# A fused transform and SwiGLU kernel: split value units from tile 3 on, the earlier order of a unit, and a broadcast row by TensorE

## The chip, the cores and the metric

The kernel runs on one core of one Trainium2 chip. The metric is the device time of one execution in microseconds (us). Five engines work side by side: TensorE (matmuls; PE in the profile, with its weight loads as PEld), VectorE (DVE), ScalarE (ACT), GpSimd (POOL) and SyncE (SP), which issues most of the transfers. [...]

## The reference

Eight batches of 3008 rows of 256 numbers go through a two-dimensional Fourier transform, of which the real part is kept. Each of the 24064 resulting rows then goes through a SwiGLU block with 1536 hidden columns:

```python
X = np.fft.fft(np.fft.fft(x, axis=1), axis=2).real      # x: (8, 3008, 256)
t = X.reshape(24064, 256)
g = t @ w_gate                                          # (256, 1536)
silu = g * (1.0 / (1.0 + np.exp(-g)))
out = (silu * (t @ w_val)) @ w_out                      # (1536, 256)
```

## The kernel before

**Mirror pairs.** The real part of the transform of row k and of row M - k consist of the same two parts, P and Q, once added and once subtracted. The kernel keeps P and Q (128 numbers each per token, since the weights take in the transform along the columns) and computes two output rows from each column of them, a plus row and a mirrored row. It folds the weights into Wp (for P), Wq (for Q) and Wm, which is -2 times Wq except in row 0. For the plus row it adds Wp.P and Wq.Q in one PSUM bank; adding Wm.Q on top gives the mirrored row in the same bank.

**Tiles and units.** The 12032 columns are cut into 24 tiles of mostly 512 columns (`wide`; tiles 0 and 3 have 480, the last one 320). A tile has 12 units, one for each 128 hidden columns (`f`). So there are 288 units, which the main loop (L874) runs over. A unit makes the gate `g` and the value `v` for the plus rows, multiplies silu(g) with v into `hp`, adds the mirror to both, and multiplies again into `hm` (with the columns reversed).

**Plain and split units.** In a plain unit the gate and the value have one bank each, TensorE runs six matmuls of 512 columns, and DVE makes both products (L755, L785). In a split unit the value is left in two parts, e (Wp.P) and o (Wm.Q), in two banks. DVE makes the values of both rows from them in three steps (L744, L746, L748); the first adds row 0 of Q, broadcast over the partitions (`bc`) and weighted by `w0`. GpSimd makes the products (L749, L773). A split unit has five matmuls of 512 columns. `split(u)` (L703) picks the units: from tile 2 to the last tile but one, f in (0, 2, 3, 5, 7, 9), and nine of twelve in tiles 21 and 22.

**Output.** The rows of a finished tile are multiplied with `w_out` while the next tile is computed: 96 matmuls of 256 columns (L675, `OWork`), eight for each unit, in two groups of four. ScalarE copies each finished pair of blocks (L681), SP stores it.

**Order of a unit, from tile 1 on** (L896 to L904): `gate_b` of the unit ahead (mirror of the gate, its silu; GpSimd's product, if split), four output matmuls, `gate_a` of this unit, `value_b` of the unit ahead (mirror of the value and product, if plain), `value_a` of this unit, four output matmuls. Tile 0 has the order of the changed kernel.

**Buffers.** [...]three for gates (`psG`), three for values (`psV`), two for outputs (`psO`). GpSimd's products have four buffers for silu results (`sgv`) and four for values (`vv`).

**Folding and transforms beside it.** GpSimd folds the rows of the next batches (L147 to L174; SDf, EOf, Af, CE, BB), in steps laid out by unit number in `seq` (L796 to L805): batch 1 in units 6 to 24, batches 2 and on from unit 25, three folds in about 62 units at first. Their loads (L128 to L141) go out three to a unit on SP. A step follows, in GpSimd's order, the products of its unit. The transforms (`transform`, L545) of a half batch run at the end of a unit named in `slot` (L788): unit 33, which is (tile 2, f = 9), then (3, 4), (5, 4), (6, 4) and so on. Each has 16 or more matmuls, two ScalarE copies into `od` and the sums into the P and Q tiles on DVE (L579).

**Row 0 of Q.** In unit 7 (10 in tile 2) of the tile ahead, two transfers on SP write row 0 of Qt to DRAM and read it back into all partitions (L881, L882).

Of the kernel before, what the change touches and what calls it, by code (L numbers as in the profile page):

```python
# [12 lines left out]
F32 = mybir.dt.float32  # L13
I32 = mybir.dt.int32
BF16 = mybir.dt.bfloat16
AF = mybir.ActivationFunctionType
Alu = mybir.AluOpType
# [14 lines left out]
def kernel(  # L32
# [8 lines left out]
    nc = tc.nc  # L41
    B, M, D = x.shape
    Dff = moe_w_gate.shape[1]
    P = 128
# [4 lines left out]
    nF = Dff // P  # L49
    T = 512  # L50
# [6 lines left out]
    nT = len(wide)  # L57
# [9 lines left out]
    def width(t):  # L67
        return wide[t]

    def tile_of(c):  # L70
        return max(t for t in range(nT) if t0[t] <= c)
# [6 lines left out]
    psG = ctx.enter_context(tc.tile_pool(name="psG", bufs=3, space=bass.MemoryType.PSUM))  # L78
# [6 lines left out]
    Wm = const.tile([P, 2, Dff], BF16, name="Wm")  # L85
# [5 lines left out]
    sel = const.tile([P, P], BF16, name="sel")  # L91
# [22 lines left out]
    def rows_at(b, row, ap):  # L114
        return bass.AP(tensor=x.tensor, offset=(b * M + row) * D, ap=ap)
# [4 lines left out]
    def down_set(b, a, j, L, n):  # L120

        return rows_at(b, R * (a + 1) - 2 * j, [[2 * L * D, n], [-2 * D, L], [1, 2 * D]])
# [107 lines left out]
    for hi in range(2):  # L230
        q.dma_start(out=XC3[64 * hi:64 * hi + NCR, 0:2, :],
                    in_=rows_at(0, 2 * (P + 1) - 1 + 2 * hi * R, [[2 * D, NCR], [R * D, 2], [1, 2 * D]]))
    for hi in range(2):
        for a in range(2):
            q.dma_start(out=XC3[64 * hi:64 * hi + NCR, 2 + a, :],
                        in_=down_set(0, 3 - 2 * hi - a, JC, LC, NC_))
    q.dma_start(out=XC0[NCR:64 + NCR + 1:64, 0:2, 1],
                in_=rows_at(0, 0, [[2 * R * D, 2], [R * D, 2], [1, D]]))
# [21 lines left out]
    for i in range(6):  # L260
        ps = psO.tile([P, T], F32, name="o")
# [99 lines left out]
    opposite(0)  # L361
    nc.vector.memset(EOf[:, 1, :, P:P + 1], 0.0)
    nc.vector.memset(Tab[:, :, :, :, NOO - 1:NOO], 0.0)
    vts(m2, pcol, scalar1=0.0, scalar2=-2.0, op0=Alu.not_equal, op1=Alu.mult)
    vts(sgn, half, scalar1=1.0 / 32, scalar2=1.0, op0=Alu.mult, op1=Alu.add)
    vts(wC, pc, scalar1=float(LC - 1), scalar2=-0.5, op0=Alu.is_equal, op1=Alu.mult)
# [146 lines left out]
    def pq_tiles(t):  # L513
        if t not in ptile:
            w = width(t) + B if t == nT - 1 else T
            ptile[t] = (pqp if t < nT - 1 else const).tile([P, w], BF16, name="Pt")
            qtile[t] = (pqp if t < nT - 1 else const).tile([P, w], BF16, name="Qt")
        return ptile[t], qtile[t]
# [78 lines left out]
    def whole_part(b, part):  # L597
        transform(b, part, (0,))
        transform(b, part, (1,))
# [15 lines left out]
    sgp = ctx.enter_context(tc.tile_pool(name="sg", bufs=3))  # L615
    sgv = ctx.enter_context(tc.tile_pool(name="sgv", bufs=4))
    esp = ctx.enter_context(tc.tile_pool(name="es", bufs=2))
    bcp = ctx.enter_context(tc.tile_pool(name="bc", bufs=2))
# [73 lines left out]
    hts = {}  # L692
    state = {}
    owork = None

    SPLIT = (0, 2, 3, 5, 7, 9)
    SPLIT_END = (0, 1, 2, 4, 5, 7, 8, 10, 11)
    t_end = tile_of((B - 1) * H) + 1

    rowd = tc.dram_tile([nT, T], BF16, name="rowd")  # L700
    bc = {}

    def split(u):  # L703

        return 2 <= u[0] < nT - 1 and u[1] in (SPLIT if u[0] < t_end else SPLIT_END)

    def gate_a(u):
        t, f = u
        w = width(t) + (B if t == nT - 1 else 0)
        fs = slice(f * P, (f + 1) * P)  # L710
        if f == 0:
            hts[t] = (hp.tile([P, nF, T + B], BF16, name="hp"), hp.tile([P, nF, T], BF16, name="hm"))
        Pt, Qt = pq_tiles(t)

        def mm(ps, Wt, gv, src, start, stop):
            nc.tensor.matmul(ps[:, :w], Wt[:, gv, fs], src[:, :w], start=start, stop=stop,  # L716
                             skip_group_check=True)

        g = psG.tile([P, T], F32, name="g")
        mm(g, Wp, 0, Pt, True, False)  # L720
        mm(g, Wq, 0, Qt, False, True)
        sg = (sgv if split(u) else sgp).tile([P, T], F32, name="sgv" if split(u) else "sg")
        nc.scalar.activation(sg[:, :w], g[:, :w], AF.Silu)  # L723
        state[u] = (g, sg)

    def value_a(u):
        t, f = u
        w = width(t) + (B if t == nT - 1 else 0)
        fs = slice(f * P, (f + 1) * P)
        Pt, Qt = pq_tiles(t)  # L730
        g, sg = state[u]

        def mm(ps, Wt, gv, src, start, stop):
            nc.tensor.matmul(ps[:, :w], Wt[:, gv, fs], src[:, :w], start=start, stop=stop,  # L734
                             skip_group_check=True)

        if split(u):
            e = psV.tile([P, T], F32, name="v")
            mm(e, Wp, 1, Pt, True, True)
            o = psV.tile([P, T], F32, name="v")  # L740
            mm(o, Wm, 1, Qt, True, True)
            stt = nc.vector.scalar_tensor_tensor
            es = esp.tile([P, T], F32, name="es")
            stt(es[:, :w], bc[t][:, :w], w0[:, f:f + 1], e[:, :w], op0=Alu.mult, op1=Alu.add)  # L744
            vp = vvp.tile([P, T], F32, name="vv")
            stt(vp[:, :w], o[:, :w], -0.5, es[:, :w], op0=Alu.mult, op1=Alu.add)  # L746
            vm = vvp.tile([P, T], F32, name="vv")
            stt(vm[:, w - 1::-1], o[:, :w], 0.5, es[:, :w], op0=Alu.mult, op1=Alu.add)  # L748
            nc.gpsimd.tensor_tensor(hts[t][0][:, f, :w], sg[:, :w], vp[:, :w], op=Alu.mult)  # L749
            state[u] = (g, vm)  # L750
            return
        v = psV.tile([P, T], F32, name="v")
        mm(v, Wp, 1, Pt, True, False)
        mm(v, Wq, 1, Qt, False, True)
        nc.vector.tensor_tensor(hts[t][0][:, f, :w], sg[:, :w], v[:, :w], op=Alu.mult)  # L755
        state[u] = (g, v)

    def mirror(u, gv, ps):
        t, f = u
        w = width(t)  # L760
        nc.tensor.matmul(ps[:, :w], Wm[:, gv, f * P:(f + 1) * P], pq_tiles(t)[1][:, :w], start=False, stop=True,  # L761
                         skip_group_check=True)

    def gate_b(u):

        t, f = u
        w = width(t)
        g, v = state[u]
        mirror(u, 0, g)
        if split(u):  # L770
            sg = sgv.tile([P, T], F32, name="sgv")
            nc.scalar.activation(sg[:, w - 1::-1], g[:, :w], AF.Silu)  # L772
            nc.gpsimd.tensor_tensor(hts[t][1][:, f, :w], sg[:, :w], v[:, :w], op=Alu.mult)  # L773
        else:
            sg = sgp.tile([P, T], F32, name="sg")
            nc.scalar.activation(sg[:, :w], g[:, :w], AF.Silu)  # L776
            state[u] = (sg, v)

    def value_b(u):
        t, f = u  # L780
        w = width(t)
        sg, v = state.pop(u)
        if not split(u):
            mirror(u, 1, v)
            nc.vector.tensor_tensor(hts[t][1][:, f, w - 1::-1], sg[:, :w], v[:, :w], op=Alu.mult)  # L785


    slot = {(b, part): max(first_tile[(b, part)] - 1, 0) * nF + 4 for b, part in jobs}  # L788
# [10 lines left out]
    for b in range(2, B, 2):  # L799
        u = slot[(b, 0)] - 1  # L800
# [8 lines left out]
    def run_loads(n):  # L809
        for _, fn in loads[:n]:  # L810
            fn()
        del loads[:n]
# [29 lines left out]
    for jb in jobs[1:]:  # L842
        u = slot[jb]
# [28 lines left out]
    prev = None  # L872
    owork = None
    for i, u in enumerate(units):  # L874
        t, f = u
        if f == (10 if t == 2 else 7) and t + 1 < nT and split((t + 1, SPLIT[0])):

            bc.pop(t - 1, None)
            bc[t + 1] = bcp.tile([P, T], BF16, name="bc")
            w = width(t + 1)  # L880
            nc.sync.dma_start(out=rowd[t + 1:t + 2, :w], in_=pq_tiles(t + 1)[1][0:1, :w])  # L881
            nc.sync.dma_start(out=bc[t + 1][:, :w], in_=rowd[t + 1:t + 2, :w].to_broadcast([P, w]))  # L882
        for fn in before.pop(i, ()):
            fn()
        if i == 10:
            loads[0:0] = ((("A", 1), fn) for fn in load_a(1, nc.sync))
        run_loads(3)

        if i < nF:
            gate_a(u)  # L890
            value_a(u)
            if prev is not None:
                gate_b(prev)
                value_b(prev)
        else:
            gate_b(prev)  # L896
            if owork:
                owork.run(4)
            gate_a(u)
            value_b(prev)  # L900
            if prev[1] == nF - 1:
                owork = OWork(prev[0], hts[prev[0]])
            value_a(u)
            owork.run(4)  # L904
        for what, j in fold_at.get(i, ()):
            fold_step(what, j, i)
        for what in act_at.pop(i, ()):
            load_next(what)
        if i in job_at:
            whole_part(*job_at[i])  # L910
        prev = u
    while owork.steps:
        owork.run(8)
    gate_b(prev)
    value_b(prev)
    owork = OWork(prev[0], hts[prev[0]])
    owork.run(len(owork.steps))

# [29 lines left out]
```

## Time and profile before

| | us |
|---|---|
| three runs | 699.02, 697.26, 696.71 |
| median | 697.26 |
| profiled execution | 699.02 |
| its span, first to last instruction | 697.2 |

| engine | busy us | share of the span |
|---|---|---|
| TensorE | 674.9 | 97% |
| TensorE weight loads | 412.4 | 59% |
| VectorE | 515.8 | 74% |
| ScalarE | 413.7 | 59% |
| GpSimd | 592.9 | 85% |

Groups (line, engine, what, form, count | busy us, mean ns of one | idle us of the engine ahead of them, and what ended it):

```profile
L749 POOL TENSOR_TENSOR hp<-sgv,vv 128x512 bf16<-128x512 f32 (+1 forms) x132 | 167.6, 1270 | 60.9 <-DVE vv L746 58.4
L785 DVE TENSOR_TENSOR hm<-sg,v 128x512 bf16<-128x512 f32 (+2 forms) x156 | 104.1, 668 | 111.9 <-PE v L761 75.8
L716 PE MATMUL g<-Pt,Wp 128*128 128x512 bf16 (+2 forms) x288 | 108.5, 377 | 0.3 <-ACT sgv L772 0.3
L153 POOL TENSOR_TENSOR SDf<-XA 128x1024 f32<-128x1024 f32 x28 | 65.9, 2360 | 2.9 <-DMA XA<-in_x_dram 2.8
```

The mean of a matmul, 377 ns, is not the time that it costs: matmuls overlap, and what counts is the distance from one start to the next. The busy share of an engine is a mean over stretches of different kind, so the tiles have to be looked at one by one.

### The profile page before, as it was taken

To read this page: it belongs to the slowest core of one execution; us is meant where nothing else is said; L and a number is where in the kernel's file an instruction comes from. 1 tells how busy PE (TensorE), PEld (TensorE's weight loads), DVE (VectorE), ACT (ScalarE), POOL (GpSimd) and SP (SyncE) were. 2 spreads that over 40 slices of the span, in tenths; PEclk is the share of its full clock that TensorE was granted. 3 is DMA by queue.
4 is the path that set the end of the run, shared out by engine and by line. 5 is a ranking of instruction groups with operands and counts; after the bars stand their busy time and mean duration, and the time that the engine had idled before them with its cause. 6 is when DMAs were issued, how large, how long until landed. Compare 5 with 4: busy or idle time off the path is not lost.

```text
span 697.2 us, 13316 instructions
## 1 busy us (share of the span) xinstructions
PE 674.9 (97%) x4348; PEld 412.4 (59%) x4348; DVE 515.8 (74%) x924; ACT 413.7 (59%) x744; POOL 592.9 (85%) x577
## 2 busy tenths in 40 slices
PE   8999879999999999999999999999999999999997
PEld 5446535566565565565665656656665556656676
DVE  8895637777777777678777787778787787788762
ACT  7675535566565566565665656655666556656663
POOL 7998988899999899999998999999899645758820
PEclk9999979999999999999999999999999999999999
DMA  9646353241512412415126111116111111101112
GB/s 223 111 72 133 99 132 91 66 129 49 157 54 71 121 54 73 118 47 166 40 62 144 54 42 44 53 40 167 39 55 46 39 36 49 54 31 55 47 46 70
DMA packets 48634, 55.33 MB, mean 79 GB/s; under 512 B 6647, under 2 KB 36532, under 8 KB 48564
## 3 DMA queue, kind: packets, MB, share of 16 engines
q1 hardware_dynamic: 45380, 52.12, 27.4%
q0 software_dynamic: 3184, 2.36, 2.5%
q8 instruction: 34, 0.56, 0.3%
q14 instruction: 36, 0.29, 0.2%
HBM read 32.14 MB, written 24.67 MB: 81 GB/s over the span
## 4 chain that ended last, share of the span: by engine, by line
PE 80%; POOL 6%; DMA 4%; issue 3%; DVE 3%; SPq 2%; ACT 1%; DVEq 0%; POOLq 0%; ACTq 0%
PE o L675 30%; PE g L716 14%; PE v L734 14%; PE g L761 8%; PE v L761 4%; DMA XA<-in_x_dram 4%; PE g L566 3%; PE v L566 3%; POOL SDf L153 2%; POOL hm L773 1%; POOL hp L749 1%; DVE vv L746 1%; DMA out_dram<-ev 1%; PE v L542 1%; PE g L542 1%
## 5 line engine op out<-in xcount | busy, mean ns | idle before, releaser
L749 POOL TENSOR_TENSOR hp<-sgv,vv 128x512 bf16<-128x512 f32 (+1 forms) x132 | 167.6, 1270 | 60.9 <-DVE vv L746 58.4
L785 DVE TENSOR_TENSOR hm<-sg,v 128x512 bf16<-128x512 f32 (+2 forms) x156 | 104.1, 668 | 111.9 <-PE v L761 75.8
L675 PE MATMUL o<-Wo,hm 128*128 128x256 bf16 (+2 forms) x1140 | 170.5, 274 | 0.0
L675 PE MATMUL o<-Wo,hp 128*128 128x256 bf16 (+2 forms) x1140 | 170.1, 273 | 0.0
L773 POOL TENSOR_TENSOR hm<-sgv,vv 128x512 bf16<-128x512 f32 (+1 forms) x132 | 167.7, 1270 | 1.7 <-ACT sgv L772 1.7
L675 PEld LDWEIGHTS <-hp 128*128 128x128 bf16 (+2 forms) x1140 | 112.0, 99 | 69.9 <-issue 14.6
L675 PEld LDWEIGHTS <-hm 128*128 128x128 bf16 (+2 forms) x1140 | 112.2, 99 | 62.5 <-issue 7.8
L776 ACT ACTIVATE sg<-g 128x512 f32<-128x512 f32 (+2 forms) x156 | 90.7, 582 | 79.7 <-PE g L761 77.8
L772 ACT ACTIVATE sgv<-g 128x512 f32<-128x512 f32 (+1 forms) x132 | 78.7, 596 | 94.2 <-PE g L761 72.5
L761 PE MATMUL g<-Qt,Wm 128*128 128x512 bf16 (+2 forms) x288 | 108.4, 376 | 12.0 <-ACT sgv L723 9.4
L716 PE MATMUL g<-Qt,Wq 128*128 128x512 bf16 (+2 forms) x288 | 108.7, 378 | 0.5 <-DVE Qt L579 0.5
L716 PE MATMUL g<-Pt,Wp 128*128 128x512 bf16 (+2 forms) x288 | 108.5, 377 | 0.3 <-ACT sgv L772 0.3
L734 PE MATMUL v<-Pt,Wp 128*128 128x512 bf16 (+2 forms) x288 | 108.8, 378 | 0.0
L755 DVE TENSOR_TENSOR hp<-sg,v 128x512 bf16<-128x512 f32 (+2 forms) x156 | 103.2, 662 | 6.8 <-ACT sg L723 5.7
L723 ACT ACTIVATE sg<-g 128x512 f32<-128x512 f32 (+2 forms) x156 | 91.5, 586 | 26.9 <-PE g L716 25.4
L746 DVE SCALAR_TENSOR_TENSOR vv<-v,es 128x512 f32<-128x512 f32 (+1 forms) x132 | 91.2, 691 | 21.9 <-POOL hp L749 4.5
L723 ACT ACTIVATE sgv<-g 128x512 f32<-128x512 f32 (+1 forms) x132 | 79.8, 604 | 34.3 <-PE g L716 22.2
L744 DVE SCALAR_TENSOR_TENSOR es<-bc,w,v 128x512 f32<-128x512 bf16 (+1 forms) x132 | 97.6, 740 | 0.3 <-PE v L734 0.3
L748 DVE SCALAR_TENSOR_TENSOR vv<-v,es 128x512 f32<-128x512 f32 (+1 forms) x132 | 89.8, 680 | 7.3 <-POOL hm L773 7.3
L153 POOL TENSOR_TENSOR SDf<-XA 128x1024 f32<-128x1024 f32 x28 | 65.9, 2360 | 2.9 <-DMA XA<-in_x_dram 2.8
L761 PE MATMUL v<-Qt,Wm 128*128 128x512 bf16 (+2 forms) x156 | 58.2, 373 | 2.0 <-DVE hp L755 2.0
L734 PE MATMUL v<-Qt,Wq 128*128 128x512 bf16 (+2 forms) x156 | 58.5, 375 | 0.0
(163 smaller groups left out, 706.8 us busy)
## 6 DMA issues: line engine op xcount, KB each, us to landing
out_dram<-ev SPq DMA_DIRECT2D x96, 128.0 KB
XA<-in_x_dram SPq DMA_DIRECT2D x32, 256.0 KB
XA<-in_x_dram SPq DMA_DIRECT2D x112, 64.0 KB
XC<-in_x_dram SPq DMA_DIRECT2D x32, 120.0 KB
XC<-in_x_dram SPq DMA_DIRECT2D x105, 32.0 KB
bc<-rowd SPq DMA_DIRECT2D x20, 128.0 KB
out_dram<-ev SPq DMA_DIRECT2D x12, 120.0 KB
out_dram<-ev SPq DMA_DIRECT2D x10, 112.0 KB
```

Of the source, the lines that this page charges most:

```text
L675: nc.tensor.matmul(ps[:n, j, :], hts[minus][:, f, c:c + n], Wo[:, f, :], start=(f == 0), stop=(f == nF - 1))
L716: nc.tensor.matmul(ps[:, :w], Wt[:, gv, fs], src[:, :w], start=start, stop=stop, skip_group_check=True)
L723: nc.scalar.activation(sg[:, :w], g[:, :w], AF.Silu)
L734: nc.tensor.matmul(ps[:, :w], Wt[:, gv, fs], src[:, :w], start=start, stop=stop, skip_group_check=True)
L744: stt(es[:, :w], bc[t][:, :w], w0[:, f:f + 1], e[:, :w], op0=Alu.mult, op1=Alu.add)
L746: stt(vp[:, :w], o[:, :w], -0.5, es[:, :w], op0=Alu.mult, op1=Alu.add)
L749: nc.gpsimd.tensor_tensor(hts[t][0][:, f, :w], sg[:, :w], vp[:, :w], op=Alu.mult)
L755: nc.vector.tensor_tensor(hts[t][0][:, f, :w], sg[:, :w], v[:, :w], op=Alu.mult)
L761: nc.tensor.matmul(ps[:, :w], Wm[:, gv, f * P:(f + 1) * P], pq_tiles(t)[1][:, :w], start=False, stop=True, skip_group_check=True)
L773: nc.gpsimd.tensor_tensor(hts[t][1][:, f, :w], sg[:, :w], v[:, :w], op=Alu.mult)
L776: nc.scalar.activation(sg[:, :w], g[:, :w], AF.Silu)
L785: nc.vector.tensor_tensor(hts[t][1][:, f, w - 1::-1], sg[:, :w], v[:, :w], op=Alu.mult)
```

## The change

The diff does four things.

1. Split units begin at tile 3 (`3 <= u[0]`). The six split units of tile 2 become plain.
2. Row 0 of Q is broadcast by a matmul: `sel`, a 128 x 128 matrix, gets ones in row 0 and zeros below; at f = 0 of each tile with split units, `sel` times the Q tile goes into a gate bank, and ScalarE copies it into `bc`, now in float32. The two transfers and the DRAM tile go.
3. The order of a unit is: gate and value of this unit (`part_a`), four output matmuls, mirrors of gate and value of the unit ahead with their silu and products (`part_b`), four output matmuls. The engines' own orders follow: on DVE the steps of this unit stand ahead of the mirrored product of the unit ahead, on GpSimd the product of this unit ahead of the mirrored one of the unit ahead, on ScalarE the silu of this unit ahead of the mirrored one of the unit ahead.
4. The pieces `gate_a`, `value_a`, `mirror`, `gate_b` and `value_b` become `part_a` and `part_b`, with the same operations in them.

```diff
+    nc.vector.memset(sel[0:1, :], 1.0)
...
-    rowd = tc.dram_tile([nT, T], BF16, name="rowd")
...
-        return 2 <= u[0] < nT - 1 and u[1] in (SPLIT if u[0] < t_end else SPLIT_END)
+        return 3 <= u[0] < nT - 1 and u[1] in (SPLIT if u[0] < t_end else SPLIT_END)
...
+    def part_a(u):
...
         g = psG.tile([P, T], F32, name="g")
         mm(g, Wp, 0, Pt, True, False)
         mm(g, Wq, 0, Qt, False, True)
...
         if split(u):
             e = psV.tile([P, T], F32, name="v")
             mm(e, Wp, 1, Pt, True, True)
             o = psV.tile([P, T], F32, name="v")
             mm(o, Wm, 1, Qt, True, True)
+            sg = sgv.tile([P, T], F32, name="sgv")
+            nc.scalar.activation(sg[:, :w], g[:, :w], AF.Silu)
...
+    def part_b(u):
...
+        for gv, ps in ((0, g), (1, v))[:1 if split(u) else 2]:
+            nc.tensor.matmul(ps[:, :w], Wm[:, gv, f * P:(f + 1) * P], Qt[:, :w], start=False, stop=True,
+                             skip_group_check=True)
         if split(u):
             sg = sgv.tile([P, T], F32, name="sgv")
             nc.scalar.activation(sg[:, w - 1::-1], g[:, :w], AF.Silu)
             nc.gpsimd.tensor_tensor(hts[t][1][:, f, :w], sg[:, :w], v[:, :w], op=Alu.mult)
+            return
+        sg = sgp.tile([P, T], F32, name="sg")
+        nc.scalar.activation(sg[:, :w], g[:, :w], AF.Silu)
+        nc.vector.tensor_tensor(hts[t][1][:, f, w - 1::-1], sg[:, :w], v[:, :w], op=Alu.mult)
...
-        if f == (10 if t == 2 else 7) and t + 1 < nT and split((t + 1, SPLIT[0])):
-
-            bc.pop(t - 1, None)
-            bc[t + 1] = bcp.tile([P, T], BF16, name="bc")
-            w = width(t + 1)
-            nc.sync.dma_start(out=rowd[t + 1:t + 2, :w], in_=pq_tiles(t + 1)[1][0:1, :w])
-            nc.sync.dma_start(out=bc[t + 1][:, :w], in_=rowd[t + 1:t + 2, :w].to_broadcast([P, w]))
+        if f == 0 and split((t, SPLIT[0])):
+            ps = psG.tile([P, T], F32, name="g")
+            w = width(t)
+            nc.tensor.matmul(ps[:, :w], sel, pq_tiles(t)[1][:, :w], start=True, stop=True)
+            bc.pop(t - 2, None)
+            bc[t] = bcp.tile([P, T], F32, name="bc")
+            nc.scalar.copy(bc[t][:, :w], ps[:, :w])
...
-        if i < nF:
-            gate_a(u)
-            value_a(u)
-            if prev is not None:
-                gate_b(prev)
-                value_b(prev)
-        else:
-            gate_b(prev)
-            if owork:
-                owork.run(4)
-            gate_a(u)
-            value_b(prev)
+        part_a(u)
+        if owork:
+            owork.run(4)
+        if prev is not None:
+            part_b(prev)
             if prev[1] == nF - 1:
                 owork = OWork(prev[0], hts[prev[0]])
-            value_a(u)
+                owork.run(4)
+        if owork and not (prev is not None and prev[1] == nF - 1):
             owork.run(4)
```

More of the change, by code (lines that the diff above doesn't have):

```diff
@@ L698 @@
     t_end = tile_of((B - 1) * H) + 1
-    rowd = tc.dram_tile([nT, T], BF16, name="rowd")
     bc = {}
     def split(u):
-        return 2 <= u[0] < nT - 1 and u[1] in (SPLIT if u[0] < t_end else SPLIT_END)
-    def gate_a(u):
+        return 3 <= u[0] < nT - 1 and u[1] in (SPLIT if u[0] < t_end else SPLIT_END)
+    def part_a(u):
         t, f = u
@@ L721, in gate_a @@
         mm(g, Wq, 0, Qt, False, True)
[L722 to L735, printed above, removed]
         if split(u):
@@ L754, in value_a @@
         mm(v, Wq, 1, Qt, False, True)
+        sg = sgp.tile([P, T], F32, name="sg")
+        nc.scalar.activation(sg[:, :w], g[:, :w], AF.Silu)
         nc.vector.tensor_tensor(hts[t][0][:, f, :w], sg[:, :w], v[:, :w], op=Alu.mult)
         state[u] = (g, v)
-    def mirror(u, gv, ps):
+    def part_b(u):
         t, f = u
         w = width(t)
[L761 to L769, printed above, removed]
+        Pt, Qt = pq_tiles(t)
+        g, v = state.pop(u)
+        for gv, ps in ((0, g), (1, v))[:1 if split(u) else 2]:
+            nc.tensor.matmul(ps[:, :w], Wm[:, gv, f * P:(f + 1) * P], Qt[:, :w], start=False, stop=True,
+                             skip_group_check=True)
         if split(u):
@@ L773, in gate_b @@
             nc.gpsimd.tensor_tensor(hts[t][1][:, f, :w], sg[:, :w], v[:, :w], op=Alu.mult)
-        else:
[L775 to L785, printed above, removed]
+            return
+        sg = sgp.tile([P, T], F32, name="sg")
+        nc.scalar.activation(sg[:, :w], g[:, :w], AF.Silu)
+        nc.vector.tensor_tensor(hts[t][1][:, f, w - 1::-1], sg[:, :w], v[:, :w], op=Alu.mult)
     slot = {(b, part): max(first_tile[(b, part)] - 1, 0) * nF + 4 for b, part in jobs}
@@ L887 @@
         run_loads(3)
-        if i < nF:
-            gate_a(u)
-            value_a(u)
-            if prev is not None:
-                gate_b(prev)
-                value_b(prev)
-        else:
-            gate_b(prev)
-            if owork:
-                owork.run(4)
-            gate_a(u)
-            value_b(prev)
+        part_a(u)
[3 more added lines that the diff above has]
+            part_b(prev)
             if prev[1] == nF - 1:
                 owork = OWork(prev[0], hts[prev[0]])
-            value_a(u)
+                owork.run(4)
+        if owork and not (prev is not None and prev[1] == nF - 1):
             owork.run(4)
@@ L913 @@
         owork.run(8)
-    gate_b(prev)
-    value_b(prev)
+    part_b(prev)
     owork = OWork(prev[0], hts[prev[0]])
```

## The prediction

> **What bounds the kernel now.** I read the share line first (TensorE 97% busy, GpSimd 85%), then the windows of the tiles of 512 tokens, cut at the first gate matmul (L716) of each, then the waits and the order of time inside the tile that falls out. Columns of the windows: the stretch, its length, busy time of PE, PEld, DVE, ACT and POOL (with instructions), granted clock, DMA share, GB/s. The lines are tiles 1, 2, 9, 14 and 22.
>
> ```profile
> 50.56:76.62 26.06, 26.06 (x170) 16.77 (x169) 16.32 (x26) 15.88 (x30) 22.55 (x26) 1.00 0.58 117
> 76.62:117.68 41.06, 32.76 (x189) 18.26 (x187) 22.38 (x43) 16.84 (x32) 38.07 (x35) 0.88 0.43 116
> 282.32:312.47 30.15, 28.42 (x181) 16.72 (x179) 21.73 (x37) 16.72 (x31) 29.99 (x28) 1.00 0.27 80
> 422.39:447.41 25.02, 25.02 (x164) 15.81 (x162) 19.39 (x31) 15.86 (x29) 23.98 (x23) 1.00 0.15 48
> 639.24:664.72 25.48, 25.04 (x161) 15.49 (x159) 21.45 (x34) 15.86 (x29) 22.26 (x19) 1.00 0.14 42
> ```
>
> Tile 14, without a transform, takes 25.02 us and TensorE never stops: that is the bound of nearly the whole run. In the trace of tile 14 a 512-column matmul starts 0.215 us after the one before it, a 256-column one 0.108 us. So a plain unit (six of 512, eight of 256) needs 2.154 us, a split unit (five) 1.939 us. Tile 1 has twelve plain units and 26.06 us, close to 12 x 2.154 = 25.85. Tile 2 is the exception: 41.06 us, 8.3 of it idle on TensorE, at a granted clock of 0.88. The first tile with split units meets a GpSimd that is still folding the next batch:
>
> ```profile
> 85.30 0.64 POOL L167 TENSOR_TENSOR CEa<-Af 128x258 bf16<-128x258 f32 x1
> 85.90 1.26 POOL L749 TENSOR_TENSOR hp<-sgv,vv 128x512 bf16<-128x512 f32 x1
> ...
> 92.52 2.35 POOL L153 TENSOR_TENSOR SDf<-XC 128x1024 f32<-128x1024 f32 x1 [2.68 <-DMA XC<-in_x_dram]
> ```
>
> The first product of tile 2 gets its turn on GpSimd at 85.90, six us after its value (L746 ended at 79.7). Later a fold step that waits for its load stands in front of the next products. ScalarE then has no free sgv buffer (there are four), and TensorE may not add the mirrored gate into a bank that ScalarE hasn't read:
>
> ```profile
> 87.19 0.60 ACT L723 ACTIVATE sgv<-g 128x512 f32<-128x512 f32 x1 [3.45 <-POOL hp L749]
> ```
>
> ```profile
> 87.84 0.58 PE L761 MATMUL g<-Qt,Wm 128*128 128x512 bf16 x1 [3.47 <-ACT sgv L723]
> ...
> 89.07 0.63 PE L716 MATMUL g<-Pt,Wp 128*128 128x512 bf16 x1
> 89.50 0.63 PE L716 MATMUL g<-Qt,Wq 128*128 128x512 bf16 x1
> ```
>
> After the stop two matmuls start 0.43 us apart, not 0.215: half clock. The waits of this stretch (us, times, longest) carry the same chain:
>
> ```profile
> ACT sgv L723 <- POOL hp L749: 7.3, 2, 3.9
> PE g L761 <- ACT sgv L723: 6.7, 2, 3.5
> ```
>
> In the steady state the order of unit 3 of tile 14 matters. The reader is to see the three DVE steps of a split unit (L744, L746, L748) with starts 0.87 and 0.61 apart, and the mirrored gate at 430.13, held 0.15 us because its silu (429.46) stood behind an output copy (429.00):
>
> ```profile
> 427.38 0.38 PE L734 MATMUL v<-Qt,Wm 128*128 128x512 bf16 x1
> ...
> 428.04 0.74 DVE L744 SCALAR_TENSOR_TENSOR es<-bc,w,v 128x512 f32<-128x512 bf16 x1
> ...
> 428.91 0.69 DVE L746 SCALAR_TENSOR_TENSOR vv<-v,es 128x512 f32<-128x512 f32 x1
> 429.00 0.58 ACT L681 COPY ev<-o 128x512 f32<-128x512 f32 x1
> ...
> 429.46 0.62 ACT L723 ACTIVATE sgv<-g 128x512 f32<-128x512 f32 x1
> 429.52 0.68 DVE L748 SCALAR_TENSOR_TENSOR vv<-v,es 128x512 f32<-128x512 f32 x1
> ...
> 430.13 0.38 PE L761 MATMUL g<-Qt,Wm 128*128 128x512 bf16 x1
> ```
>
> [...]the bc issue follows its rowd issue by 1.1 us and more on SP (302.30 and 303.43).
>
> **The change, part by part.** The profiled execution took 699.02 us, its span is 697.2; the median of three is 697.26. Differences below are made on the span and put on the median, since 1.8 us around the span stay.
>
> 1. *Tile 2 becomes plain.* GpSimd loses 12 products (6 of L749, 6 of L773, starts 1.22 us apart: 14.6 us), TensorE gains six matmuls. DVE trades 6 x 2.08 us for 12 x 0.60 and is idle enough. The tile should cost what tile 1 costs, 26.06, and the transform of unit (2, 9), 3.2 (tile 10, unit 4: 5.13 from gate to gate, less 1.94): 29.26. Saved: 41.06 - 29.26 = **-11.8**. What is late next? The fold steps up to unit 35 (13.2 us by their rows, once the XC load has landed at 92.5) end near 105.7; tile 3 starts at 76.6 + 29.3 = 105.9 and wants its first product at about 108.4. The stall doesn't move there.
>
> 2. *Broadcast row by TensorE.* 20 matmuls with sel, 0.215 each, on the bound: **+4.3**. The 20 ScalarE copies (priced by L681, 0.58, 11.6 us in all) run between two silus of an engine that is 59% busy; their result is there as early as the e matmul two behind it needs. If that cover failed, 0.1 to 0.6 each would show. L744 with an f32 row instead of bf16: 0.69 to 0.74 (L746 and L744), nothing on TensorE. The memset of one row of sel: 0.06 by L362, before DVE waits for the first placed rows: 0 to 0.1. SP loses two issues a tile and the wait between them, some 1.7 us; behind them stand loads and output stores that no TensorE wait ends on outside tile 2: 0, at best -0.5.
>
> 3. *Order of a unit.* Now: mirrored gate of the unit ahead, four output matmuls, gate, mirrored value of the unit ahead, value, four. After: gate, value, four, both mirrors of the unit ahead, four. The same matmuls, so only waits change. DVE's order turns round too: the mirrored product hm of the unit ahead (0.60) comes after the three steps of a split unit.
>  - Mirrored gate behind silu: it now comes a whole unit after its silu. The 0.15 us holds at units 3 and 6 (steps of 2.10 instead of 1.95) go: -0.30 a tile, 18 tiles: **-5.4**.
>  - Unit 3 after split unit 2 and plain unit 1. By the built order the second value bank of unit 3 waits for L748's counterpart of unit 2. Set the start of unit 2 to 0: its e matmul starts at 0.43, DVE at 0.92 (0.49 after a matmul's start, as 427.43 against 426.94), the third step ends at 0.92 + 1.48 + 0.68 = 3.08. Unit 2 lasts 2.154, and the matmul is due at 2.154 + 0.645 = 2.80. With 0.05 for the signal: 0.33 late, 18 tiles: **+5.9**.
>  - Unit 0: its second value bank waits for hm of unit 10, which ends 3.05 after the start of unit 11; due at 3.01 with the sel matmul: 0.07, 20 times: **+1.4**. The other banks have 1 us and more to spare: units 5, 7 and 9 take a bank 1.1 to 1.5 us after its release. The gate bank of unit 0 is free 0.01 before it is due.
>  - After a transform the gate comes at once and not 0.65 later; the Pt sums that free its bank end 0.45 to 0.6 us earlier (541.66 against 542.11): 0.
>  - Tiles 21 and 22 (nine split units): three waits of 0.33 each, against 1.5 us lost now in tile 22 (25.48 less 9 x 1.939 + 3 x 2.154 = 23.91): -0.5 to +0.5, taken as 0.
>
> 4. *GpSimd near its limit.* Tiles 4, 5, 8 and 9 lose 0.3, 0.9, 0.9 and 1.7 us now (each against 25.02, or 28.40 with a transform), where POOL is 99% busy. After the change hm of a split unit is ready one unit (2 us) later, which shortens what may queue there; against it the mirrored gate no longer hangs on the newest silu, so a late sgv buffer reaches TensorE about a unit later. The trace can't show which wins: -4 to +5. I take 0.
>
> Sum: -11.8 + 4.3 - 5.4 + 5.9 + 1.4 = **-5.6**, so 697.26 - 5.6 = 691.7.
>
> **The rivals.**
>  - *As summed* (0.50): 691.7, own range 688.5 to 695.
>  - *The new order also hides the lag of GpSimd* (0.17): the 3.8 us of part 4 go too, 688. For it: the stops in tile 2 ran through the mirrored gate alone. Against: GpSimd's work is the same, and 29.99 of 30.15 us in tile 9 can't shrink.
>  - *GpSimd's lag takes the place of tile 2's stall* (0.20): the fold steps are a load away from tile 3, and hm is late. 5 us more: 696.7. For it: POOL at 99% in four tiles, and the load's landing at 92.5. Against: 2.7 us of margin at tile 3, and TensorE itself is 0.2 us a tile slower.
>  - *Slower: DVE becomes the pacer of the value banks* (0.13). In five places of each split tile (units 0, 3, 5, 7, 9) a bank is freed by DVE, which in the new order reaches hm only after 2.08 us of split steps. Four have 1 us of margin by my count. If the transforms' sums (2.1 us of DVE a time), late vv buffers and bank hand-overs eat it, each place costs up to 0.3: 100 x 0.15 = 15, 706.7. It decides from 0.08 us a place on (7.7 us). For it: DVE's steps before hm are as long as a unit. Against: DVE is 77% busy in tile 14.
>  - That the edit doesn't do what it says I exclude: the built order has no split product in tile 2.
>
> **How the numbers follow.** No change means within 0.3% (695.2 to 699.4), about what a measurement of this kernel can tell. Faster: all of the first two cases and 0.06 of the third, 0.73. Same: 0.14 of the third. Slower: 0.13. The range leaves out the upper part of the slow case and the far end of the second: 686 to 699.
>
> **What would show it.** Tile 2 near 29 us with POOL no longer between TensorE and its mirrors, at clock 1.00; twenty L856 matmuls; unit 3 about 0.33 us over its 1.94; steady tiles 25.1 to 25.4. Wrong would be: a tile 2 over 32, a stop of several us at the start of tile 3, or tiles without a transform over 25.7, with value matmuls waiting for DVE.

## The result and the profile after

| | before | after |
|---|---|---|
| median, us | 697.46 (696.71 to 699.02, 4 runs) | 687.67 (687.24 to 688.74, 4 runs) |
| profiled execution, us | 699.02 | 687.24 |
| its span, us | 697.2 | 685.5 |

After/before is 0.986, 95% interval 0.984 to 0.988: 9.8 us faster on the medians, 11.7 on the two spans. Each pair of numbers below is from the two profiled executions; that of before lay 1.6 us above its median, that of after 0.4 below.

The share line of the page of after (engine, busy us, share, instructions):

```profile
PE 672.8 (98%) x4374; PEld 414.2 (60%) x4374; DVE 514.6 (75%) x919; ACT 432.9 (63%) x764; POOL 579.1 (84%) x565
```

Shares say little: PE rose by one point (97% to 98%). The windows of after, cut at the first gate matmul of tiles 1, 2, 9, 14 and 22, as shown of before:

```profile
50.35:75.91 25.56, 25.56 (x166) 16.32 (x165) 16.97 (x26) 16.24 (x29) 21.69 (x24) 1.00 0.62 126
75.91:105.38 29.47, 29.45 (x195) 17.89 (x193) 18.97 (x37) 17.42 (x32) 24.64 (x26) 1.00 0.52 131
269.42:298.05 28.63, 28.54 (x180) 16.82 (x179) 21.54 (x37) 17.68 (x31) 28.47 (x28) 1.00 0.28 81
408.85:434.10 25.25, 25.16 (x165) 15.93 (x164) 19.50 (x31) 16.77 (x29) 24.45 (x24) 1.00 0.13 43
627.71:652.55 24.84, 24.55 (x159) 15.54 (x159) 21.15 (x33) 16.39 (x29) 22.30 (x18) 1.00 0.14 43
```

Tile 2 fell from 41.06 to 29.47 at a granted clock of 1.00 (0.88 before), with GpSimd busy for 24.6 us of it and no longer for 38.1. Tile 9 lost its stop (30.15 to 28.63) although GpSimd is as full as before (28.47 of 28.63). Tile 14 is 0.23 us longer. All 24 tiles, from gate to gate, summed up:

| tiles | change, us |
|---|---|
| 0 and 1 | -0.7 |
| 2 | -11.6 |
| 3 to 20, at 0.23 each (the value of tile 14 and of most others) | +4.1 |
| what 5, 8 and 9 gained beyond that: -1.1, -0.9, -1.7 | -3.7 |
| 21, 22, 23 | +0.3 |

The sum is -11.6 of the 11.7. In the first and last row 0.4 is only moved: in the new order four output matmuls of a tile come behind the first gate of the next one, so the window of tile 1 has four fewer and what follows tile 23 has four more.

GpSimd at the turn from tile 2 to tile 3, in the timeline of after (start, duration, engine, line; in brackets the idle time before and what ended it):

```profile
100.93 2.35 POOL L153 TENSOR_TENSOR SDf<-XC 128x1024 f32<-128x1024 f32 x1
107.91 1.21 POOL L736 TENSOR_TENSOR hp<-sgv,vv 128x480 bf16<-128x480 f32 x1 [4.63 <-DVE vv L733]
```

The last fold step before tile 3 ends at 103.3, and GpSimd then waits 4.63 us for the first value of tile 3. So the stop did not move to tile 3.

Unit 3 of tile 14 (the gate of unit 2 starts at 413.02, that of unit 3 at 415.19), in the timeline of after:

```profile
413.45 0.38 PE L716 MATMUL v<-Pt,Wp 128*128 128x512 bf16 x1
...
413.87 0.75 DVE L731 SCALAR_TENSOR_TENSOR es<-bc,w,v 128x512 f32<-128x512 f32 x1 [0.73 <-PE v L716]
...
415.36 0.68 DVE L735 SCALAR_TENSOR_TENSOR vv<-v,es 128x512 f32<-128x512 f32 x1
...
415.62 0.38 PE L716 MATMUL v<-Pt,Wp 128*128 128x512 bf16 x1
...
415.88 0.60 ACT L728 ACTIVATE sgv<-g 128x512 f32<-128x512 f32 x1 [0.55 <-PE g L716]
...
416.09 0.38 PE L716 MATMUL v<-Qt,Wm 128*128 128x512 bf16 x1
```

The second value matmul of unit 3 should come 0.215 after the first and comes 0.47 after it: DVE's third step for unit 2 (L735) ends at 416.04 and frees the bank. That is the new wait of 0.26. The mirrored gate of unit 3, which before hung on its silu, now comes behind the gate, the value and four output matmuls of unit 4, at 418.70: nothing waits for the silu at 415.88.

In tile 9 the lag of GpSimd is still there, but it ends at ScalarE and VectorE. Timeline of after:

```profile
279.25 1.28 POOL L758 TENSOR_TENSOR hm<-sgv,vv 128x512 bf16<-128x512 f32 x1
279.27 0.38 PE L753 MATMUL g<-Qt,Wm 128*128 128x512 bf16 x1
...
279.48 0.60 PE L676 MATMUL o<-Wo,hp 128*128 128x256 bf16 x4
...
279.92 0.48 PE L567 MATMUL v<-Tab,BBa 128*128 128x376 bf16 x2
...
280.55 0.60 ACT L757 ACTIVATE sgv<-g 128x512 f32<-128x512 f32 x1 [1.32 <-POOL hm L758]
280.55 0.69 DVE L735 SCALAR_TENSOR_TENSOR vv<-v,es 128x512 f32<-128x512 f32 x1 [1.71 <-POOL hm L758]
```

ScalarE stands 1.32 us for a free sgv buffer and VectorE 1.71 us for a free vv buffer, and TensorE goes on with output and transform matmuls. In the same place the kernel before stopped TensorE:

```profile
291.15 0.60 ACT L723 ACTIVATE sgv<-g 128x512 f32<-128x512 f32 x1 [1.65 <-POOL hp L749]
...
291.80 0.38 PE L761 MATMUL g<-Qt,Wm 128*128 128x512 bf16 x1 [1.73 <-ACT sgv L723]
```

### The profile page after: what moved, and what is told of

Read it like the earlier page. It is cut to its first block, busy times and chain, and to the rows that moved or that the text cites. A ratio compares the mean times of both kernels' runs of the same rounds, so it can differ in the third digit from the quotient of the medians.

```text
span 685.5 us, 13259 instructions
## 1 busy us (share of the span) xinstructions
PE 672.8 (98%) x4374; PEld 414.2 (60%) x4374; DVE 514.6 (75%) x919; ACT 432.9 (63%) x764; POOL 579.1 (84%) x565
## 4 chain that ended last, share of the span: by engine, by line
PE 89%; DVE 5%; issue 2%; POOL 2%; ACT 0%; DVEq 0%; ACTq 0%; POOLq 0%
PE o L676 34%; PE v L716 17%; PE g L716 16%; PE g L753 9%; PE v L753 4%; PE g L567 3%; PE v L567 3%; DVE vv L735 3%; DVE vv L733 1%; PE v L543 1%; PE g L543 1%; PE g L856 1%; PE g L421 1%; PE v L421 1%; PE o L430 0%
## 5 line engine op out<-in xcount | busy, mean ns | idle before, releaser
L736 POOL TENSOR_TENSOR hp<-sgv,vv 128x512 bf16<-128x512 f32 (+1 forms) x126 | 160.1, 1272 | 54.3 <-DVE vv L733 42.4
L758 POOL TENSOR_TENSOR hm<-sgv,vv 128x512 bf16<-128x512 f32 (+1 forms) x126 | 159.6, 1272 | 8.5 <-ACT sgv L757 8.1
L744 DVE TENSOR_TENSOR hp<-sg,v 128x512 bf16<-128x512 f32 (+2 forms) x162 | 107.9, 666 | 33.2 <-ACT sg L743 32.4
L731 DVE SCALAR_TENSOR_TENSOR es<-bc,w,v 128x512 f32<-128x512 f32 (+1 forms) x126 | 93.7, 744 | 50.5 <-PE v L716 50.3
L762 DVE TENSOR_TENSOR hm<-sg,v 128x512 bf16<-128x512 f32 (+2 forms) x162 | 107.4, 663 | 24.1 <-ACT sg L761 14.4
L761 ACT ACTIVATE sg<-g 128x512 f32<-128x512 f32 (+2 forms) x162 | 94.7, 585 | 45.6 <-PE g L753 45.4
L743 ACT ACTIVATE sg<-g 128x512 f32<-128x512 f32 (+2 forms) x162 | 94.4, 583 | 45.0 <-PE g L716 43.5
L757 ACT ACTIVATE sgv<-g 128x512 f32<-128x512 f32 (+1 forms) x126 | 75.3, 598 | 47.4 <-PE g L753 41.1
L728 ACT ACTIVATE sgv<-g 128x512 f32<-128x512 f32 (+1 forms) x126 | 75.1, 596 | 40.3 <-PE g L716 35.5
L733 DVE SCALAR_TENSOR_TENSOR vv<-v,es 128x512 f32<-128x512 f32 (+1 forms) x126 | 87.0, 690 | 17.6 <-PE v L753 1.0
L735 DVE SCALAR_TENSOR_TENSOR vv<-v,es 128x512 f32<-128x512 f32 (+1 forms) x126 | 85.7, 680 | 2.7 <-POOL hm L758 2.7
L716 PEld LDWEIGHTS <-Wp 128*128 128x128 bf16 x576 | 56.2, 98 | 41.0 <-issue 4.2
L682 ACT COPY ev<-o 128x512 f32<-128x512 f32 x90 | 52.7, 586 | 30.8 <-PE o L676 28.2
```

## The experiments

Four parts of the change can be told apart: where split units begin, the row, the order of a unit, and GpSimd's backlog. Every kernel computes the whole reference. The start of the main loop differs between the profiled executions (first value matmul at 26.0 to 27.7 us; the reason wasn't looked for), so tiles are compared one by one.

### Each half alone

The kernel before with the new first tile only:

```diff
-        return 2 <= u[0] < nT - 1 and ...
+        return 3 <= u[0] < nT - 1 and ...
```

> The kernel before with split units from tile 3 on and nothing else changed. If the six split units of tile 2 are the whole of the stall there, tile 2 falls from 41.06 us to about 29.3 and the time to about 685.7. On tiles 5, 8 and 9 two theories part: if the new order of a unit is what took GpSimd's lag off TensorE, they keep 29.3, 25.9 and 30.1 us as before the change; if the relief of GpSimd in tile 2 did it, they fall to about 28.4, 25.0 and 28.4 and the time to about 682.

Measured: 689.59 us (688.00 to 690.46), ratio to before 0.989 (0.986 to 0.992). Tile 2 takes 29.58, so this edit alone makes 11.5 of the 11.6 there. Tiles 5, 8 and 9 keep their stops (29.28, 25.81, 30.28). Tile 3 is 0.85 longer than before. The time is 3.9 above the 685.7 expected; tile 3 and a main loop that starts 1.4 later in the profiled execution are part of it, the rest isn't explained. Waits of TensorE and of VectorE in this run (us in all, times, longest):

```profile
PE g L761 <- ACT sgv L723: 2.9, 3, 1.9
```

```profile
DVE es L744 <- DMA bc<-rowd: 1.1, 1, 1.1
```

The first line is the old chain, without tile 2. The second is new: with a shorter tile 2 the row of tile 3, read back from DRAM, comes too late.

The changed kernel with split units from tile 2 on:

```diff
-        return 3 <= u[0] < nT - 1 and ...
+        return 2 <= u[0] < nT - 1 and ...
```

> The changed kernel with split units from tile 2 on, so only the order of a unit and the broadcast by TensorE differ from the kernel before. If tile 2's stall comes from GpSimd's queue whatever the order, tile 2 stays near 40 us and the time near 698 (687.7 + 11). If the new order takes up GpSimd's lag there too, as it seems to do in tiles 5, 8 and 9, tile 2 is several us shorter and the time 692 to 695.

Measured: 694.15 us (693.04 to 695.40, 20 runs), ratio 0.995 (0.994 to 0.997). Tiles 5, 8 and 9 take 28.43, 25.25 and 28.63, as in the changed kernel: the relief in tile 2 has no part in their gain. Its tile 2 (window) and the longest waits of TensorE:

```profile
77.53:113.11 35.58, 30.21 (x185) 17.82 (x188) 22.00 (x43) 17.64 (x32) 35.11 (x36) 0.95 0.45 118
```

```profile
PE v L716 <- DVE vv L735: 4.0, 3, 2.0
```

Two of the three, 3.5 us in all, lie in tile 2. VectorE, in turn, waits for a vv buffer that GpSimd's products free (waits of VectorE):

```profile
DVE vv L735 <- POOL hm L758: 5.2, 5, 2.0
...
DVE vv L735 <- POOL hp L736: 2.8, 1, 2.8
```

The new order takes 5.5 us off a tile 2 with split units (41.06 to 35.58); the other 6.1 need plain units. With as much backlog as here the new order stops too, but by another way: the value banks wait for DVE, and DVE for GpSimd.

### The row

The changed kernel with the two transfers in place of the matmul with `sel`:

```diff
-        if f == 0 and split((t, SPLIT[0])):
-            ps = psG.tile([P, T], F32, name="g")
-            nc.tensor.matmul(ps[:, :w], sel, pq_tiles(t)[1][:, :w], start=True, stop=True)
...
-            nc.scalar.copy(bc[t][:, :w], ps[:, :w])
+        if f == (10 if t == 2 else 7) and t + 1 < nT and split((t + 1, SPLIT[0])):
...
+            nc.sync.dma_start(out=rowd[t + 1:t + 2, :w], in_=pq_tiles(t + 1)[1][0:1, :w])
+            nc.sync.dma_start(out=bc[t + 1][:, :w], in_=rowd[t + 1:t + 2, :w].to_broadcast([P, w]))
```

> The changed kernel with the broadcast row by the two transfers of the kernel before (bf16, one tile ahead). If the 20 matmuls stand on TensorE's path at 0.215 us each, 4.3 us less: about 683.4, and unit 11 to unit 0 falls from 2.38 us to 2.17. If the gate bank that the matmul takes costs more than that, more; if the matmuls fill gaps, nothing changes.

Measured: 689.71 us (686.79 to 691.25, 5 runs), ratio 0.991 (0.987 to 0.994): not faster than the changed kernel, and 6.3 above the 683.4 of the first case. The profiled execution, span 685.0, is the fastest of the five. Tile 14 still takes 25.25. Tiles 5, 8 and 9 take 28.43, 25.25 and 28.64 here too, so their gain is the order's and not the row's. The start of its unit 0 with the matmul (timeline of after):

```profile
408.63 0.38 PE L856 MATMUL g<-Qt,sel 128*128 128x512 bf16 x1
...
409.28 0.38 PE L716 MATMUL v<-Pt,Wp 128*128 128x512 bf16 x1
...
409.55 0.38 PE L716 MATMUL v<-Qt,Wm 128*128 128x512 bf16 x1
```

and without it (timeline of this run):

```profile
409.15 0.69 DVE L762 TENSOR_TENSOR hm<-sg,v 128x512 bf16<-128x512 f32 x1 [0.40 <-ACT sg L761]
...
409.40 0.38 PE L716 MATMUL v<-Pt,Wp 128*128 128x512 bf16 x1
...
409.89 0.38 PE L716 MATMUL v<-Qt,Wm 128*128 128x512 bf16 x1
```

The second value matmul waits for the bank that DVE's hm of unit 10 frees (409.15 + 0.69 = 409.84). With `sel` it comes 0.27 after the first, without `sel` 0.49. So the matmul's 0.215 only fills a wait: leaving it out shortens nothing in such a tile. It does in tile 21 (28.45 instead of 28.99; more on this below), and tiles 2 and 4 are 0.2 and 0.3 shorter. Against that, tile 3 is 0.95 longer with the transfers:

```profile
103.50 0.24 SPq L858 DMA_DIRECT2D rowd<-Qt  x1
...
104.89 0.35 SPq L859 DMA_DIRECT2D bc<-rowd  x1
...
107.89 0.71 DVE L731 SCALAR_TENSOR_TENSOR es<-bc,w,v 128x480 f32<-128x480 bf16 x1 [2.10 <-DMA bc<-rowd]
```

The second issue, at 104.89, comes 1.15 us after the end of the first (103.50 + 0.24), and the row is in place 3.0 us later, 4.4 after the first issue. What SP waits for between the two can be read in the trace of before: the second issue (L882) waits for the first transfer all 21 times, 23.8 us in all and 1.9 at most.

### More buffers for the lag

If only the lag of GpSimd mattered, deeper buffers should do what the new order does. The kernel before, and the first run (first tile 3), each with:

```diff
-    sgv = ctx.enter_context(tc.tile_pool(name="sgv", bufs=4))
+    sgv = ctx.enter_context(tc.tile_pool(name="sgv", bufs=6))
...
-    vvp = ctx.enter_context(tc.tile_pool(name="vv", bufs=4))
+    vvp = ctx.enter_context(tc.tile_pool(name="vv", bufs=5))
```

> The kernel before with six silu buffers for GpSimd's products instead of four and five value buffers instead of four; nothing else. If TensorE stops in tile 2 because those buffers are full while GpSimd folds, room for one more split unit takes up some 4 us of each of the stops: tile 2 falls from 41.06 us to 33 to 37, and tiles 8 and 9 lose their stops (25.9 to 25.0, 30.1 to 28.4). If the stops come from GpSimd's work as such, the times stay within 1 us.

Measured: 693.68 us (691.00 to 696.54, 20 runs), ratio 0.994 (0.993 to 0.996). As the first case expected, tile 2 falls to 35.29 and tiles 8 and 9 to 25.15 and 28.40. Not expected was that tile 10 rises from 28.20 to 31.86, and tile 5 keeps its stop (29.55, before 29.27). Waits of the weight loads:

```profile
PEld L675 <- POOL hp L749: 1.8, 2, 1.2
PEld L566 <- POOL CEa L166: 1.3, 2, 0.7
...
PEld L566 <- POOL CEa L167: 1.0, 2, 0.5
```

> The kernel before with split units from tile 3 on and the same extra buffers. Tiles 5, 8 and 9 kept their stops when split units began at tile 3 in the old order (29.28, 25.81, 30.28 us) and lost them in the new order. If the new order helps because a late silu buffer reaches TensorE a unit later, more buffers do the same in the old order: 28.4, 25.0, 28.4, 3.5 us less than the 689.6 of split units from tile 3 alone. If it is DVE's or GpSimd's turn in the order that helps, the stops stay.

Measured: 688.56 us (686.99 to 690.34), ratio 0.988 (0.984 to 0.993), no clear difference from the run with the old buffers. Tiles 8 and 9 lose their stops (25.02, 28.40), tiles 5 and 10 take 31.03 and 30.37. By the waits, what is late now is next in line: the folded coefficients of a transform (CEa) and the products that the output matmuls read (L675). That deeper queues of products hold them up is the likely reading; it wasn't tested by itself.

### The mirrored gate's place

The changed kernel, with the mirrored gate of the unit ahead, its silu and GpSimd's product moved ahead of this unit's gate:

```diff
+        if prev is not None:
+            gate_b(prev)
         part_a(u)
         if owork:
             owork.run(4)
         if prev is not None:
-            part_b(prev)
+            value_b(prev)
```

> The changed kernel with one thing moved: the mirrored gate of the unit ahead, its silu and GpSimd's mirrored product come ahead of the gate of this unit instead of behind its value and four output matmuls. Everything else stays: tile 3, the row by TensorE, DVE's three steps ahead of the mirrored product hm of a plain unit. Theory A, the mirrored gate's early place is what lets GpSimd's lag stop TensorE: tiles 5, 8 and 9 lose about 0.7, 0.7 and 1.5 us again, near 29.1, 26.0 and 30.1 us, and waits of the mirrored gate for a silu in a sgv buffer come back; the time is about 3 us over that of the changed kernel, 690 to 691. Theory B, it is the order on VectorE, or the order of the two products on GpSimd with the value banks: the three tiles stay at 28.4, 25.3 and 28.6 us and the time within 1 us of 687.7.

Measured: 692.61 us (691.43 to 693.73, 6 runs), ratio 0.994 (0.992 to 0.996). The changed kernel beside it:

> The changed kernel once more, on the same chip as the run beside it, as its measure: 687 to 689 us, tiles 5, 8 and 9 at 28.4, 25.3 and 28.6 us under either theory.

Measured: 687.15 us (686.89 to 688.45), ratio 0.987 (0.984 to 0.989); tiles 5, 8 and 9 at 28.42, 25.24 and 28.63. With the gate early they take 29.28, 25.19 and 29.70: tile 5 loses 0.9, tile 9 1.1 of its 1.5, tile 8 nothing. The lengths alone mislead here. In tile 9 (timeline):

```profile
281.07 1.03 PE L676 MATMUL o<-Wo,hp 128*128 128x256 bf16 x8
...
282.42 0.60 ACT L728 ACTIVATE sgv<-g 128x512 f32<-128x512 f32 x1 [1.61 <-POOL hp L736]
...
283.07 0.38 PE L752 MATMUL g<-Qt,Wm 128*128 128x512 bf16 x1 [0.96 <-ACT sgv L728]
```

ScalarE's wait for a sgv buffer stops TensorE again, by the chain of the kernel before. So for tile 9 Theory A holds. In the changed kernel the mirrored gate comes later by four matmuls of 512 and four of 256, 1.3 us in tile 14 (from 417.40, the gate of unit 4, to 418.70), and that, as an estimate, is the lag it forgives. (The run moves the mirrored silu and GpSimd's mirrored product along with the gate, so it doesn't tell their places apart.) Waits of TensorE in this run, whole execution:

```profile
PE g L716 <- ACT sg L761: 2.7, 4, 0.7
...
PE g L752 <- ACT sgv L728: 1.0, 1, 1.0
```

The second line is tile 9, and it is the only wait of its kind. The first line is another, not foreseen: the first gate after a transform waits until ScalarE's mirrored silu has read its bank. It comes once each in tiles 2, 5, 10 and 13 (in tile 5 at 176.78, while in the kernel before tile 5 stood at the mirrored gate of unit 3). So tile 5 is longer for this reason, and not by Theory A. In tiles 5 and 8 the old stop doesn't come back though the gate is early: there it is not the gate's place alone that frees TensorE. What else does wasn't tried.

The median is 5.5 us above that of the changed kernel where 3 were expected, the profiled span 6.1. Of the span 1.1 come from tile 9, 3.2 from tiles 2, 5, 10 and 13, 1.8 from tile 0; 1.6 lie ahead of tile 0, where the executions differ by as much for other kernels too. The other tiles are up to 0.35 shorter, 1.5 in all.

### Other places for the split units

The wait of 0.26 comes from two split units in a row (2 and 3). Alternating them, `SPLIT = (0, 2, 4, 6, 8, 10)` in place of `(0, 2, 3, 5, 7, 9)`, first with the row by transfer:

> As the run with the row by transfers, and split units at f = 0, 2, 4, 6, 8, 10 instead of 0, 2, 3, 5, 7, 9 (same number, no two side by side) in tiles 3 to 20. If the wait of unit 3 for a value bank (2.21 us instead of 1.95) comes from two split units side by side, it goes: 18 times 0.26 is 4.7 us, about 678.7. If it comes from DVE's load in general, it moves to another unit and the time stays at 683.4.

Measured: 684.52 us (682.48 to 686.00), ratio 0.982 (0.978 to 0.986), 5.8 above the 678.7 expected. Tile 14 takes 24.73 and has no wait left, so the first case holds there. Tile 3 takes 32.1, tile 5 29.96, tile 9 28.89, tile 10 28.94; the row of tile 3 is 4 us late, and in unit 1 of tiles 5 and 10 the output matmuls wait for GpSimd's last products of the tile before, which come later now that unit 10 is split. Waits of DVE and of the weight loads:

```profile
DVE es L731 <- DMA bc<-rowd: 4.0, 1, 4.0
```

```profile
PEld L675 <- POOL hp L736: 3.3, 2, 2.2
```

Then with the row by TensorE:

> The changed kernel with split units at f = 0, 2, 4, 6, 8, 10 in tiles 3 to 20 (same number). The waits of unit 3 (0.26 us) and of unit 0 (0.07 beside the broadcast matmul) go and the broadcast matmul stands on the path: 24.94 us in a tile without a transform instead of 25.25, 18 times 0.31, 5.6 us less, about 682. If the stops that the alternate form showed with the row by transfers (tile 3: 32.05 us, tile 5: 29.96) were the late row, tile 3 is 27.5; if GpSimd's, tile 3 stays over 30.

Measured: 689.00 us (687.71 to 689.07), ratio 0.989 (0.985 to 0.992): no gain, where about 682 was expected. Tile 3 is back at 27.8, but tile 14 takes 25.19, and tiles 5 and 10 are 1.1 and 0.3 longer than in the changed kernel. Timeline, end of tile 14:

```profile
435.50 0.60 ACT L757 ACTIVATE sgv<-g 128x512 f32<-128x512 f32 x1 [0.55 <-PE g L753]
...
435.68 0.38 PE L856 MATMUL g<-Qt,sel 128*128 128x512 bf16 x1
...
436.09 0.59 ACT L859 COPY bc<-g 128x512 f32<-128x512 f32 x1
436.15 0.38 PE L716 MATMUL g<-Pt,Wp 128*128 128x512 bf16 x1
```

`sel` takes one of the three gate banks, so the gate of unit 0 needs that of unit 10, which is free when its mirrored silu ends at 436.10. The matmul costs 0.47 here, 0.25 of it this wait: unit 10 is now split, and with no mirrored value behind it its mirrored gate stands 0.215 nearer to the gate of unit 0. So the expected gain fails on a bank. The changed kernel has this wait in one place, ahead of tile 22, since in tile 21 unit 10 is split: the matmul starts at 627.24 and the gate at 627.71, again 0.47.

Last, the row by TensorE for tile 3 alone, where the transfer is late, and by transfer a tile ahead for all others (`bc` in bf16 in all tiles):

```diff
-        if f == 0 and split((t, SPLIT[0])):
+        if f == 0 and t == 3:
...
+        if f == 7 and 3 < t + 1 < nT and split((t + 1, SPLIT[0])):
+            bc.pop(t - 1, None)
+            bc[t + 1] = bcp.tile([P, T], BF16, name="bc")
...
+            nc.sync.dma_start(out=rowd[t + 1:t + 2, :w], in_=pq_tiles(t + 1)[1][0:1, :w])
+            nc.sync.dma_start(out=bc[t + 1][:, :w], in_=rowd[t + 1:t + 2, :w].to_broadcast([P, w]))
```

> As the run before it, with the row by a matmul for tile 3 alone and by two transfers for the later tiles, a tile ahead. Tile 3 has no stop, and the later tiles lose 0.215 us each, since no wait is left for the broadcast matmul to fill: 24.72 us, 17 times 0.215 or 3.7 us less than with the matmul everywhere, about 678.5. If the transfers come late in other tiles too, part of it is lost there.

Measured: 682.09 us (681.33 to 682.48), ratio 0.979 (0.975 to 0.983), span 679.6; tile 3 27.39, tile 14 24.73. It beats both kernels: its interval lies below that of the changed kernel (0.984 to 0.988). It is 3.6 above the 678.5 expected. Tiles 5 and 10 keep their new stops (29.98 and 28.96), and tile 9 has one too (28.90): a matmul of its transform waits 0.74 us for a value bank that DVE's third step, late behind GpSimd, frees (281.37). Tiles with a transform of the same kind and no stop take 27.90 (for 5 and 10) and 28.11 (for 9), so the three stops make 2.1, 1.1 and 0.8, about what is missing.

## Why the prediction was right, point by point

The direction and the main part, tile 2, were right by the mechanism that was named. The number was not: 691.7 was said, and 687.67 lies below the likeliest case's own range (688.5 to 695), at the 688 of the second rival, which had 0.17. The whole range, 686 to 699, holds the result because it made room for that rival.

1. **Tile 2, -11.8: right.** It measured -11.6, and -11.5 with the edit of the first tile alone. The XC load landed at 90.0, the fold steps ended at 103.3 and the first product of tile 3 came at 107.9, where 92.5, 105.7 and 108.4 were written. The granted clock of before was 0.50 from 87.84 to 89.00, right behind the stop of 3.47 us; in after TensorE is busy for 29.45 of the 29.47 us of tile 2.
2. **The row by TensorE, +4.3: the term is wrong, its sum with another holds.** The matmul alone costs nothing in the steady tiles, since unit 0 would wait for hm of unit 10 in any case: per tile, 0.215 + 0.07 with it and 0.28 (0.49 less 0.215) without it. The prediction added 0.07 beside the matmul and so got the right 0.28 for the pair, but priced the edit by itself at 4.3. Ahead of tile 22 it costs 0.47. The freed SP was priced at 0 to -0.5, but for a row that comes late there was no term: with a short tile 2 the transfers would cost 0.85 to 0.95 in tile 3. The trace of before can't show it, since tile 2 is long there.
3. **The order of a unit.** The two silu waits of 0.15 went (-5.4: right; units 3 and 6 have none left, and no wait of the mirrored gate is listed in after). Unit 3's bank wait came where it was said, 0.26 instead of 0.33, so about +4.7 and not +5.9: DVE started 0.42 after the first value matmul (413.45 to 413.87), where 0.49 was set. The 0.05 for the signal is what the trace shows (416.04 to 416.09). The 0.49 was read from an hm step, which takes longer to start (last section). Unit 0's 0.07 came nearly as said (409.55 is 0.27 after 409.28, so 0.06). The gate bank of unit 0, "free 0.01 before it is due", did hold in the steady tiles, but not ahead of tile 22. Per steady tile +0.23 measured, +0.315 summed. Tiles 21 and 22 gave +0.54 and -0.64, within their -0.5 to +0.5 together, the +0.54 by the row's matmul.
4. **GpSimd near its limit, taken as 0: wrong in size.** Tiles 5, 8 and 9 gained 3.7 us; tile 4 nothing (unit 3's bank wait is 0.61 there instead of 0.26, at 140.69, since DVE's steps for unit 2 come late). This is the second rival. Its sentence that a late sgv buffer reaches TensorE about a unit later is what the run with the early gate shows for tile 9 (1.3 us later, and not a whole unit); for tiles 5 and 8 the cause within the new order stays open. The argument against it, that a tile with 29.99 us of GpSimd in 30.15 can't shrink, was false. GpSimd is busy nearly throughout tile 9 in both kernels (29.99 of 30.15 us, 28.47 of 28.63), so its busy time there falls with the length of the tile; what it hasn't done by then it does later (in tile 11 its busy time rises from 24.09 to 25.17).

With the measured sizes (-11.6 for tile 2, +4.7 for unit 3, +1.1 for unit 0, -3.7 for part 4, the rest as it stood) the sum is -10.6. The other 1.0 of the 11.6 between the two profiled executions lies in tiles 0, 1 and 21 to 23. On the medians the gain is 9.8. The third and fourth rivals didn't happen: GpSimd was idle at the start of tile 3, and of the five places where DVE frees a bank only two wait in a steady tile, units 0 and 3, for which part 3 had sums. (So three had margin in the prediction's own sums, not the four that the rival counts.)

## What to carry to other kernels

When an engine lags at times, look at how late its lag may reach the engine that sets the time: in tile 9, 1.3 us more between a gate and its mirror kept GpSimd's lag from TensorE. Three more buffers (two for silu results, one for values) freed tiles 8 and 9 as well, but other tiles then waited longer for GpSimd (tile 10 by 3.7 us). Price an added instruction on the bounding engine together with the bank waits around it: the same matmul cost 0 us behind one layout and 0.47 behind another. When an expected stop seems to come back, look which instruction waits, and not only how long the tile is. A stop that is removed early can make a small transfer late that it had covered: with a short tile 2, DVE waited 1.1, 2.1 and 4.0 us for the row of tile 3 in three of the runs that had it by transfer there.

## What was not expected of the hardware

- A row of 0.9 KB through DRAM and back took 4.4 and 5.1 us from the first issue to its use in tile 3 (the run with the row by transfers, and the one with alternating split units too), of which 1.4 and 2.1 us passed before the second transfer was issued on SP.
- The hand-over from TensorE to VectorE took two values. DVE's first step of a split unit starts 0.42 us after the start of the value matmul that it waits for at unit 2 of tile 14 (413.45 to 413.87), and 0.50 after it at unit 0 (409.28 to 409.78). In the trace of after, 20 of the 126 first steps, those of unit 0, which also need ScalarE's copy into `bc`, have a waiting instruction of their own ahead of them (0.02 us long), and it is this one that waits for TensorE's signal. DVE starts 0.02 us after that signal without it (65 first steps) and 0.10 to 0.12 after it with it (19 first steps). Where the row came by transfer and was long in place, unit 0 shows no lag: in the last experiment, ten first steps in a row (399.68 to 436.77, more than a tile, so unit 0 is among them) all start after a wait of 0.76 for the value matmul. All 156 hm steps of before have such a waiting instruction as well, and those that wait for TensorE start 0.09 us after its signal at the median; this is the step from which the prediction took its 0.49, though ScalarE's part, the silu that ended at 426.88, had been done for 0.5 us. Timeline of before, then of after:

```profile
426.94 0.38 PE L761 MATMUL v<-Qt,Wm 128*128 128x512 bf16 x1
...
427.43 0.69 DVE L785 TENSOR_TENSOR hm<-sg,v 128x512 bf16<-128x512 f32 x1 [0.76 <-PE v L761]
```

```profile
409.78 0.75 DVE L731 SCALAR_TENSOR_TENSOR es<-bc,w,v 128x512 f32<-128x512 f32 x1 [0.28 <-PE v L716]
```

The 0.07 by which the wait of unit 3 came out shorter is this difference.
